# Chunk-selected attention and top-1 routing: the attention loop written out engine by engine

## The chip, the cores and the metric

The program runs on one core of one Trainium2 chip. Its time is the device time of one execution in microseconds (us); the figure for a kernel is the median of its timed runs. The profile is one further execution, seen by the hardware profiler; its span (first to last instruction) is a few us shorter than the device time of the same execution. Engines are named as the profile names them: PE is the matrix engine (PEld its weight loads), DVE the vector engine, ACT the scalar engine, POOL the general engine, SP the one that issues plain transfers.

## The reference

Attention over 4 batches, 8 heads, 768 positions, 64 dimensions, in which each query may look only at the 6 best of 24 chunks of 32 keys; then a mixture of 8 experts of which each token goes to one.

```python
k_min, k_max = min and max of k over each chunk of 32 keys
ub = sum_d max(q*k_min, q*k_max)                 # one bound per query and chunk
ub = where(causal chunk, ub, -1e9); top_chunks = the 6 largest
scores = q @ k.T / 8, kept where the key's chunk is chosen and key <= query
attn = softmax(scores); out = attn @ v           # (4, 8, 768, 64)

x = out as (3072, 512)                           # heads side by side
logits = x @ w_gate; e = argmax(logits); g = softmax(logits)[e]
result[token] = g * relu(x @ w1[e]) @ w2[e]      # (3072, 512)
```

## The kernel before

The attention is done in 16 steps, one for each *pair* of heads (four pairs make a batch). A pair's work is cut into 7 score units; `u` 0 and 1 belong to the first 384 queries, 2 to 6 to the second. Units 1 and 6 have two parts, 256 and 128 queries wide; the others are 384 wide. Scores are computed as keys x queries, exponentiated, cut by the causal mask on POOL, and then used in two ways: as moving operand of the product with v ("AV", `po`), and summed on DVE into an accumulator `acc`, whose column sums give the softmax denominator.

```python
def scores(i, u):                                # 128 columns (keys) at once, bf16
    kte, qsb = KTE[i % 2], QSB[i % 2]            # two key buffers, two query buffers
    ps = ps_s.tile([128, 2, 512], FP32)          # ps_s: two of these
    for (kb, w, c0) in parts: for hd in range(2):
        matmul(pv[:, hd, :], lhsT=kte[:, hd, ts(kb, 128)], rhs=qsb[:, hd, w queries])
    for each part: nc.scalar.activation(P, pv, AF.Exp)
    on diagonal blocks: nc.gpsimd.affine_select(P ...)      # causal

def attend(i, u):                                # 64 columns (dimensions of v), fp32
    for parts, hd: matmul(po[64*hd:64*hd+64, ...], lhsT=vt[:, kb, hd, :], rhs=P[:, hd, ...])
    if last: ot = copy of po (DVE)
    if not first: for parts: nc.vector.tensor_tensor(acc, acc, P, ALU.add)

def ud(i):                                       # 32 columns, fp32
    for hd, hf: matmul(pu[32*(2*hd+hf):+32], lhsT=dcol, rhs=acc[hf][:, hd, :])   # denominators
    for hd, hf: matmul(pu[32*(2*hd+hf):+32], lhsT=wgb[:, hp, hd], rhs=ot[hf])    # gate logits
```

Beside these a pair needs: transposes of its keys (`k0`, `k1`), of its queries (`q0`, `q1`), of the chunk bounds (`select`), of `ud` (`lgp`) and of the two outputs (`x0`, `x1`), all 128-column fp32 transposes in threes; transposes of the chunk mask (`mask`, 64 columns, bf16); and the bounds themselves:

```python
def kse(): KS = kmx + kmn; KD = kmx - kmn        # DVE
def q_e(hf):
    qT = copy of pt (DVE); qA = Abs(pt) (ACT)
    QSB head 0 <- qT (POOL); QSB head 1 <- pt (ACT)
def ub(): pu = KS.T @ qT + KD.T @ qA             # 64 columns, fp32; twice the reference's bound
```

All transposes and `ub`, `ud` share three PSUM buffers (`ps_m`). The loop runs PE in written order; DVE, ACT and POOL are ordered by a scheduler. Pair `i` is interleaved with the preparation of pairs `i+1` and `i+2` and with the outputs of `i-1` and `i-2`:

```python
groups = [(0, 1), (2, 3), (4, 5), (6,)]
for i in range(16):
    for g in range(4):
        g 0: scores(i, 2); scores(i, 3); x1 of i-2
        g 1: scores(i, 4); scores(i, 5); select of i+1; (second pair of a batch) rank
        g 2: scores(i, 6); k0 of i+2; mask of i+1
        g 3: lgp, x0 of i-1; scores(i+1, 0); scores(i+1, 1); k1, q0, q1 of i+2; load k, q, v of i+3
        for u in groups[g]: attend(i, u)
        g 0: ub of i+1; (second pair) logits        g 1: ud of i-1
        (second pair of a batch) g 2: scatter(0, 2, 4)   g 3: scatter(1, 3, 5)
        now and then: load_w of 512 KB of expert weights (POOL queue)
```

Every fourth pair, when a batch is complete, its tokens are routed: `logits` (11 small DVE operations), `rank` (12 small matmuls, 6 small DVE operations) and six scatters of token rows to DRAM (POOL queue). The row buffers `xrow` are three; a batch needs two, so the second buffer of a batch is the one from which the previous batch's scatters 0, 2, 4 read.

After the loop come 28 expert tiles of 128 tokens. A tile is gathered (POOL queue), transposed by a transfer (SP queue), and goes through `up` (8 matmuls of 512 columns), a relu on ACT, a second transfer-transpose, `down` (8 more), a scaling on ACT, and a scatter to the output. The first 11 tiles hold rows of the first three batches and may be gathered before the last batch is routed:

```python
gather(0..3), x_in(0..3) in the last pair; then
up(0); ud; gather(4); up(1); lgp, x0, x1, logits; gather(5); up(2); down(0); rank; gather(6)
scatter(0..5 of the last batch); table(False)
for j in 3..: gather(j + 4); up(j); x_in(j + 3); down(j - 2)
```

Of the kernel before, what the change touches and what calls it, by code (L numbers as in the profile page):

```python
# [24 lines left out]
def kernel(  # L25
# [33 lines left out]
    DC = E  # L59
    NU = 7  # L60
# [36 lines left out]
    wgb = const.tile([128, HP, 2, 32], FP32)  # L97
    tokid = const.tile([128, B, 2, 3], I32)
    warm = const.tile([128, 1], FP32)
    KTE, QSB, KS, KD = [], [], [], []  # L100
    for i in range(2):
        KTE.append(buf.tile([128, 2, S], BF16, name=f"KTE{i}"))
        QSB.append(buf.tile([128, 2, S], BF16, name=f"QSB{i}"))
        KS.append(buf.tile([128, 64], FP32, name=f"KS{i}"))
        KD.append(buf.tile([128, 64], FP32, name=f"KD{i}"))
    nsel = buf.tile([128, 3, 2, 2, 32], BF16, name="nsel")
    colc = work.tile([128, S], BF16, tag="Pa", bufs=4, name="colc")
# [43 lines left out]
    def consts_pool():  # L151
# [3 lines left out]
        zero_half(QSB[1])  # L155
        nc.gpsimd.memset(ones_b[:], 1.0)
# [9 lines left out]
    def consts_last():  # L166
# [3 lines left out]
        nc.sync.dma_start(out=wgb[0:64, :, 0, 0:E], in_=wg_v[0:64])  # L170
        nc.sync.dma_start(out=wgb[64:128, :, 1, 0:E], in_=wg_v[64:128])
# [21 lines left out]
    def load(i):  # L193
        b, hp = divmod(i, HP)
        for nm, src in (("k", k), ("q", q), ("v", v)):
            t_ = ld.tile([128, NT, 2, D], FP32, tag=nm, bufs=2 if nm == "v" else 1)
            for hd in range(2):
                nc.sync.dma_start(out=t_[:, :, hd, :],
                                  in_=src[b, 2 * hp + hd].rearrange("(t p) d -> p t d", p=128))
            st[i][nm] = t_  # L200

    def prep_steps(i):
        s = st[i]
        kte, qsb, ks, kd = KTE[i % 2], QSB[i % 2], KS[i % 2], KD[i % 2]
        kmx = {}
# [7 lines left out]
        def k_e(hf):  # L213
            if hf == 0:
                s["kmx"] = work.tile([128, NCH], FP32, tag="kmx", name="kmx")
                s["kmn"] = work.tile([128, NCH], FP32, tag="kmn", name="kmn")
            pt = s[f"kp{hf}"]
            pk = pt[:].rearrange("p (c w) -> p c w", w=CH)
            nc.vector.tensor_reduce(s["kmx"][:, ts(hf, 12)], pk, AX.X, ALU.max)
            nc.vector.tensor_reduce(s["kmn"][:, ts(hf, 12)], pk, AX.X, ALU.min)  # L220
            nc.scalar.activation(kte[0:64, 0, ts(hf, 384)], pt[0:64, :], AF.Copy, bias=0.0, scale=0.125)  # L221
            nc.scalar.activation(kte[0:64, 1, ts(hf, 384)], pt[64:128, :], AF.Copy, bias=0.0, scale=0.125)

        def k_half(hf):
            k_t(hf)
            k_e(hf)
# [7 lines left out]
        def q_e(hf):  # L234
            pt = s[f"qp{hf}"]
            qT = work.tile([128, 384], FP32, tag=f"qT{hf}")
            qA = work.tile([128, 384], FP32, tag=f"qA{hf}")
            nc.vector.tensor_copy(out=qT[:], in_=pt[:])  # L238
            nc.scalar.activation(qA[:], pt[:], AF.Abs)
            nc.gpsimd.tensor_copy(out=qsb[0:64, 0, ts(hf, 384)], in_=qT[0:64, :])  # L240
            nc.scalar.activation(qsb[0:64, 1, ts(hf, 384)], pt[64:128, :], AF.Copy)
            s[f"qT{hf}"], s[f"qA{hf}"] = qT, qA

        def first():
            s["kmx"] = work.tile([128, NCH], FP32, tag="kmx", name="kmx")
            s["kmn"] = work.tile([128, NCH], FP32, tag="kmn", name="kmn")
            pk = [ps_m.tile([128, 384], FP32, tag="m", name="pk") for _ in range(2)]
            pq = [ps_s.tile([128, 2, 512], FP32, tag="s", name="pq") for _ in range(2)]
            for p_, nm in ((pk, "k"), (pq, "q")):
                for hf in range(2):  # L250
                    dst = p_[hf][:, 0, :] if nm == "q" else p_[hf]
                    for t in range(3):
                        nc.tensor.transpose(dst[:, ts(t, 128)], s[nm][:, 3 * hf + t], ident_f[:])

            def k_red(hf):
                v_ = pk[hf][:].rearrange("p (c w) -> p c w", w=CH)
                nc.vector.tensor_reduce(s["kmx"][:, ts(hf, 12)], v_, AX.X, ALU.max)
                nc.vector.tensor_reduce(s["kmn"][:, ts(hf, 12)], v_, AX.X, ALU.min)

            def k_out(hf, hd):  # L260
                nc.scalar.activation(kte[0:64, hd, ts(hf, 384)], pk[hf][64 * hd:64 * hd + 64, :],
                                     AF.Copy, bias=0.0, scale=0.125)

# [6 lines left out]
            for hf in range(2):  # L270
                s[f"qT{hf}"] = work.tile([128, 384], FP32, tag=f"qT{hf}", name="qT")
                s[f"qA{hf}"] = work.tile([128, 384], FP32, tag=f"qA{hf}", name="qA")
                nc.scalar.activation(s[f"qA{hf}"][:], pq[hf][:, 0, 0:384], AF.Abs)
                nc.vector.tensor_copy(out=s[f"qT{hf}"][:], in_=pq[hf][:, 0, 0:384])
                nc.gpsimd.tensor_copy(out=qsb[0:64, 0, ts(hf, 384)], in_=s[f"qT{hf}"][0:64, :])
            for hf in range(2):
                nc.scalar.activation(qsb[0:64, 1, ts(hf, 384)], pq[hf][64:128, 0, 0:384], AF.Copy)
            k_out(1, 1)

        def select_first():  # L280
# [3 lines left out]
            prep[1]["k0t"]()  # L284
# [29 lines left out]
            scores(0, 0)  # L314
            scores(0, 1)
# [306 lines left out]
    XB = 8  # L622
# [223 lines left out]
```

## Time and profile before

| | us |
|---|---|
| device time, median of 3 (381.53 to 382.80) | 382.76 |
| span of the profiled execution | 375.4 |
| PE busy | 340.7 |
| ACT busy | 236.3 |
| DVE busy | 230.9 |
| POOL busy | 178.3 |
| first AV matmul starts at | 24.5 |
| `ud` of the second-to-last pairs start at (from the matrix engine's timeline) | 241.34, 254.19 |
| first expert matmul starts at | 260.7 |

The table is read from the page's first part and from the timeline of PE. PE is the busiest engine, but its busy time is modelled, and it includes every gap that is shorter than the modelled tail of a matmul; how long a group of matmuls really holds PE is better read from the *starts* in the timeline: the start of the next group minus its own. In the page's strip of 40 slices one slice is 9.4 us, somewhat less than one pair.

Starts of `ud` give the pair's period. In order, from the timeline, the steps between them are 14.48, 14.19, 14.19, 14.68, 16.49, 14.18, 14.19, 14.67, 18.19, 14.18, 14.18, 14.68, 18.10, 12.84 and 8.34 us: a steady 14.2, with a longer step in each of three pairs, those in which a batch is routed.

### The profile page before, as it was taken

The numbers are of one execution on the slowest core, as the hardware profiler recorded it, in microseconds if no ns is written. First come the engines' busy times: TensorE is split into PE (matmuls) and PEld (weight loads), VectorE is DVE, ScalarE is ACT, GpSimd is POOL, SyncE is SP. The second block draws the span as 40 slices with busy tenths as digits, with TensorE's granted clock in tenths as the row PEclk, the third lists the DMA queues.
The fourth block names the chain that finished last, engine by engine and source line by source line (L and its number), as shares of the span: only waits on it lengthen the run. The fifth ranks groups of instructions, "written<-read, shape, count | busy, mean of one in ns | idle before, by whom it ended". The sixth has DMA issues, their size and how long they took to land.

```text
span 375.4 us, 7367 instructions
## 1 busy us (share of the span) xinstructions
PE 340.7 (91%) x2233; PEld 171.5 (46%) x2233; DVE 230.9 (61%) x789; ACT 236.3 (63%) x398; POOL 178.3 (47%) x299
## 2 busy tenths in 40 slices
PE   6778999999988999998999997988997899999980
PEld 3334455465554554553545544443543444444430
DVE  7378798898997888996889898876430000000000
ACT  4467697797785977975779779461453345454430
POOL 3422352352476433548334428467177565555331
PEclk9759999999999999998999999899999999999996
DMA  9455989989979989869898993515799999899750
GB/s 181 73 110 88 182 157 154 190 165 164 177 158 200 181 156 189 164 130 197 158 211 150 167 197 75 113 34 123 97 220 193 248 227 194 202 203 194 183 140 28
DMA packets 138182, 59.81 MB, mean 159 GB/s; under 512 B 122779, under 2 KB 130973, under 8 KB 138144
## 3 DMA queue, kind: packets, MB, share of 16 engines
q1 hardware_dynamic: 120608, 29.91, 42.5%
q0 software_dynamic: 17536, 29.42, 40.2%
q8 instruction: 20, 0.33, 0.3%
q14 instruction: 18, 0.15, 0.1%
HBM read 56.14 MB, written 10.51 MB: 178 GB/s over the span
## 4 chain that ended last, share of the span: by engine, by line
PE 54%; ACT 13%; DVE 10%; issue 9%; DMA 7%; POOL 4%; SPq 1%; POOLq 0%; ACTq 0%; DVEq 0%
PE po L408 14%; PE ps L386 7%; PE ph L659 7%; PE pu L330 6%; PE py L675 5%; ACT Pr L391 3%; PE pt L468 3%; DMA xg<-xs_dram,grow 3%; PE pu L436 3%; ACT QSB L359 3%; ACT QSB L358 3%; PE pu L441 3%; PE pt L231 2%; POOL out_dram L680 2%; DVE Pa L420 2%
## 5 line engine op out<-in xcount | busy, mean ns | idle before, releaser
L420 DVE TENSOR_TENSOR Pa<-Pa,Pr 128x768 f32<-128x768 f32 (+2 forms) x112 | 82.2, 734 | 2.7 <-POOL Pr L395 1.6
L395 POOL TENSOR_SCALAR_AFFINE_SELECT Pr<-Pr 128x256 f32<-128x256 f32 x80 | 34.2, 446 | 73.7 <-ACT Pr L391 72.7
L391 ACT ACTIVATE Pr<-ps 128x768 f32<-128x768 f32 (+2 forms) x112 | 65.3, 628 | 3.5 <-PE ps L386 2.0
L675 PE MATMUL py<-w_all,hT 128*128 x224 | 52.8, 379 | 1.4 <-DMA hT<-h__4677 1.2
L386 PE MATMUL ps<-QSB,KTE 128*128 128x384 bf16 (+2 forms) x288 | 49.4, 296 | 2.0 <-ACT QSB L359 1.1
L680 POOL DMA_INDIRECT out_dram<-y,ti x28 | 27.8, 993 | 38.0 <-ACT y L679 32.5
L386 PEld LDWEIGHTS <-KTE 128*128 128x128 bf16 x288 | 24.4, 99 | 33.9 <-issue 26.1
L675 PEld LDWEIGHTS <-hT 128*128 128x128 bf16 x224 | 21.9, 98 | 28.2 <-DMA hT<-h__4677 1.6
L533 POOL DMA_INDIRECT xs_dram<-xrow,sli x24 | 26.4, 1101 | 13.8 <-DVE sli L526 5.2
L659 PE MATMUL ph<-w_all,KTE 128*128 x120 | 28.4, 379 | 3.6 <-DMA KTE<-xg 3.3
L444 ACT ACTIVATE ud<-pu 128x384 f32<-128x384 f32 x16 | 7.9, 491 | 35.0 <-PE pu L441 32.5
L391 ACT ACTIVATE Pa<-ps 128x768 f32<-128x768 f32 x32 | 26.0, 811 | 2.3 <-PE ps L386 1.6
L659 PE MATMUL ph<-w_all,QSB 128*128 x104 | 24.6, 379 | 0.0
L186 POOL DMA_DIRECT2D w_all<-in_moe_w_dram x32 | 24.4, 762 | 0.0
L240 POOL CAST QSB<-qT 64x384 bf16<-64x384 f32 x30 | 14.9, 505 | 14.3 <-DVE qT L238 13.9
L647 DVE TENSOR_TENSOR ti<-xg,inv_i 128x1 int32<-128x1 int32 x9 | 1.5, 172 | 30.4 <-DMA xg<-xs_dram,grow 30.4
L470 DVE TENSOR_TENSOR xrow<-pt,rec 128x384 bf16<-128x384 f32 x32 | 17.6, 552 | 4.1 <-DMA xs_dram<-xrow,sli 3.3
L659 PEld LDWEIGHTS <-KTE 128*128 128x128 bf16 x120 | 11.6, 98 | 18.2 <-DMA KTE<-xg 3.1
L630 POOL DMA_INDIRECT xg<-xs_dram,grow x16 | 16.9, 1057 | 4.8 <-issue 3.5
L413 DVE COPY ot<-po 128x384 f32<-128x384 f32 x32 | 17.7, 554 | 2.4 <-PE po L408 2.2
L679 ACT ACTIVATE y<-py,xg 128x512 f32<-128x512 f32 x16 | 11.0, 687 | 12.8 <-PE py L675 10.4
L221 ACT ACTIVATE KTE<-pt 64x384 bf16<-64x384 f32 x30 | 14.5, 483 | 6.2 <-DVE kmn L220 5.8
(317 smaller groups left out, 654.6 us busy)
## 6 DMA issues: line engine op xcount, KB each, us to landing
w_all<-in_moe_w_dram POOLq DMA_DIRECT2D x32, 512.0 KB, 7.2
out_dram<-y,ti POOLq DMA_INDIRECT x28, 3.7
t__119<-in_k_dram SPq DMA_DIRECT2D x2, 192.0 KB, 3.2
t__122<-in_q_dram SPq DMA_DIRECT2D x2, 192.0 KB, 3.9
t__125<-in_v_dram SPq DMA_DIRECT2D x2, 192.0 KB, 4.3
t__134<-in_v_dram SPq DMA_DIRECT2D x2, 192.0 KB, 4.2
t__128<-in_k_dram SPq DMA_DIRECT2D x2, 192.0 KB, 3.4
t__131<-in_q_dram SPq DMA_DIRECT2D x2, 192.0 KB, 4.1
```

Of the source, the lines that this page charges most:

```text
L186: d = nc.gpsimd.dma_start(out=dst, in_=src.rearrange("(c p) f -> p c f", p=128))
L330: nc.tensor.matmul(pu[64 * hf:64 * hf + 64, :], lhsT=w_[:], rhs=s[f"{nm}{hf}"][:], start=(nm == "qT"), stop=(nm == "qA"), skip_group_check ...
L386: nc.tensor.matmul(pv[:, hd, :], lhsT=kte[:, hd, ts(kb, 128)], rhs=qsb[:, hd, ds(qb * 384 + 384 - w, w)], start=True, stop=True, skip_grou ...
L391: nc.scalar.activation(P[:, :, ds(c0, w)], pv, AF.Exp)
L395: nc.gpsimd.affine_select(out=pd, in_=pd, pattern=[[0, 2], [1, 128]], compare_op=ALU.is_ge, fill=0.0, base=0, channel_multiplier=-1)
L408: nc.tensor.matmul(po[64 * hd:64 * hd + 64, 384 - w:384], lhsT=vt[:, kb, hd, :], rhs=P[:, hd, ds(c0, w)], start=first, stop=last and n == ...
L413: nc.vector.tensor_copy(out=ot[:], in_=po[:])
L420: nc.vector.tensor_tensor(acc[:, :, 384 - w:384], acc[:, :, 384 - w:384], P[:, :, ds(c0, w)], ALU.add)
L533: d = nc.gpsimd.indirect_dma_start(out=xs_dram[:], out_offset=bass.IndirectOffsetOnAxis(ap=sli[:, u:u + 1], axis=0), in_=bst[b][f"xrow{u % ...
L659: nc.tensor.matmul(ph[:, fh, :], lhsT=xT[:, c, :], rhs=w_all[:, ds(wo + (c * F + fh * 512), 512)], start=(c == 0), stop=(c == NDC - 1), sk ...
L675: nc.tensor.matmul(py[:], lhsT=hT[:, c, :], rhs=w_all[:, ds(wo + (W1W + c * DM), DM)], start=(c == 0), stop=(c == NFC - 1))
L680: d = nc.gpsimd.indirect_dma_start(out=out[:], out_offset=bass.IndirectOffsetOnAxis(ap=fs[j]["ti"], axis=0), in_=y[:], in_offset=None, bou ...
```

## The change

Six things are done, and all of them in the attention loop or at the seam behind it.

1. **Scores on 64-column tiles.** Each score matmul is split in two, 64 keys each, written to the lower and upper half of the PSUM tile; they then have the same column width as AV.
2. **A new order of PE.** Scores and AV alternate unit by unit; the 128-column transposes are collected in three visits per pair: keys; then `ud`, output and bounds; then output and queries. Preparation is split into steps so that PE, DVE and ACT parts can be placed apart.
3. **Written order on DVE and ACT too** in the loop, not PE alone; in the expert part too.
4. **Three key buffers** instead of two.
5. **Work moved.** Unit 6 is no longer added to the accumulator on DVE; `ud` sums it with further `dcol` matmuls, and needs only two gate matmuls, as both heads' gate columns now stand side by side in `wgb`. The bound is rewritten as k_min·q + (k_max - k_min)·relu(q): `KS` is a copy, and relu(q) is made on POOL from `qT`, where |q| was made on ACT.
6. **The seam.** `logits` moves to the first pair after a batch, `rank` to the start of the second; scatters go out one per slot; eight tiles are gathered in the last pair instead of four; the last batch's scatters go out two at a time between expert tiles; k, q and v are loaded separately, each as its buffer is freed.

The core of the diff, with cuts marked:

```diff
-    for i in range(2):
+    for i in range(3):
         KTE.append(buf.tile([128, 2, S], BF16, name=f"KTE{i}"))
...
-            nc.scalar.activation(qA[:], pt[:], AF.Abs)
+            nc.gpsimd.tensor_scalar(qA[:], qT[:], 0.0, None, ALU.max)
...
-                nc.vector.tensor_tensor(ks[r, c], s["kmx"][r, :], s["kmn"][r, :], ALU.add)
+                nc.vector.tensor_copy(out=ks[r, c], in_=s["kmn"][r, :])
...
-                nc.tensor.matmul(pv[:, hd, :], lhsT=kte[:, hd, ts(kb, 128)],
-                                 rhs=qsb[:, hd, ds(qb * 384 + 384 - w, w)], ...)
+                for c in range(0, 128, CW):                     # CW = 64
+                    nc.tensor.matmul(pv[c:c + CW, hd, :], lhsT=kte[:, hd, ds(kb * 128 + c, CW)],
+                                     rhs=qsb[:, hd, ds(qb * 384 + 384 - w, w)], ...)
... (ud)
+            for n, (kb, w, c0) in enumerate(parts):             # parts of unit 6
+                for hd in range(2):
+                    if n == 0:
+                        mm(2 * hd, wgb[:, hp, :], s[f"ot{hd}"][:], start=False, stop=True)
+                    mm(2 * hd + 1, dcol[:], s["P6"][:, hd, ds(c0, w)], w, ...)
... (the loop; cut: k, q, v loads, weights, first and last pairs)
+            av(i - 1, 6); out_t(i - 1, 1); scores(i, 0); scores(i, 1)
+            r["ud"](); pn["q_v"](1); scatters(i, 0)
+            if hp == 1 and b > 0: route[b - 1]["rank"]()
+            keys(j, lambda: scores(i, 2))                       # visit 1
+            if hp == 1 and b > 0: route[b - 1]["rank_v"]()
+            av(i, 0); scores(i, 3); scatters(i, 1); av(i, 1); add(i, 1); out_t(i, 0)
+            pn["ub"](); pj["kse"](); scatters(i, 2)
+            r["lgp_t"](); r["x_t"](0); pn["select_t"]()         # visit 2
+            r["lgp"](); r["xr"](0); pn["select"]()
+            scores(i, 4); av(i, 2); scores(i, 5); av(i, 3); scatters(i, 3)
+            scores(i, 6); add(i, 3)
+            if hp == 0 and b > 0: route[b - 1]["logits"]()
+            r["x_t"](1); pj["q_t"](0); pj["q_t"](1)             # visit 3
+            r["xr"](1); add(i, 4); scatters(i, 4)
+            pn["mask"](); av(i, 4); pj["q_v"](0); pj["q_s"](0); pj["q_s"](1)
+            add(i, 5); av(i, 5); scatters(i, 5)
... (expert tiles)
-                    if lo == 0 and j + 4 < hi:
-                        gather(j + 4)
+                    if lo == 0 and j + 5 < hi:
+                        if late:
+                            r["scatter"](late[:2]); del late[:2]
+                        gather(j + 5)
```

Here `r` stands for the outputs of pair i-1, `pn` for the preparation of i+1, `pj` for that of i+2, `hp` for the pair's place in its batch (0 to 3); `xr(hf)` multiplies the transposed output by the reciprocal denominators into `xrow`, on DVE.

## The prediction

> **What bounds the kernel now.** I read the page's strip first, then busy time by stretch, then the PE timeline of one steady pair, then the stretches that are longer.
>
> ```profile
> PE   6778999999988999998999997988997899999980
> PEclk9759999999999999998999999899999999999996
> ```
>
> PE is busy nearly everywhere; the 7 and 5 at the left are the start-up, and its granted clock dips twice more, at the two 8s (around 170 and 240 us), which are batch seams. Busy time by stretch: a steady pair, then one in which a batch is routed (columns: stretch, its length, busy us of PE, PEld, DVE, ACT, POOL, PE clock, DMA share, GB/s).
>
> ```profile
> 133.16:147.35 14.19, 14.11 (x111) 7.57 (x109) 12.53 (x40) 11.64 (x21) 5.30 (x13) 1.00 0.91 168
> 162.02:180.21 18.19, 16.04 (x111) 8.07 (x109) 13.90 (x48) 11.83 (x21) 12.65 (x17) 0.91 0.85 176
> ```
>
> In the steady pair PE has no hole, DVE is at 88% (12.53 of 14.19), ACT at 82%: PE sets the pace. So I ask what PE's 14.19 us consist of (start, modelled us, group; I subtract starts).
>
> ```profile
> 138.11 0.82 PE L386 MATMUL ps<-QSB,KTE 128*128 128x384 bf16 x6
> 138.77 0.52 PE L210 MATMUL pt<-ident_f,t__1772 128*128 128x128 f32 x3
> ...
> 142.64 0.82 PE L408 MATMUL po<-Pr,t__1570 128*64 128x256 f32 x8
> 143.29 0.82 PE L330 MATMUL pu<-qT,KS 128*64 128x384 f32 x4
> 143.94 0.82 PE L330 MATMUL pu<-qA,KD 128*64 128x384 f32 x4
> 144.69 0.84 PE L386 MATMUL ps<-QSB,KTE 128*128 128x384 bf16 x4
> 145.43 0.55 PE L338 MATMUL pt<-ident_f,ubT 128*128 128x128 f32 x3
> 145.91 0.87 PE L408 MATMUL po<-Pa,t__1570 128*64 128x384 f32 x4
> 146.60 0.81 PE L408 MATMUL po<-Pr,t__1570 128*64 128x384 f32 x4
> ```
>
> Units: one AV unit 0.65 (142.64 to 143.29); two score units 0.66 (138.11 to 138.77), so 0.33 each; `ub` 2 x 0.65. The second half of `ub` takes 0.75 (143.94 to 144.69) where the first took 0.65: leaving 64 columns for 128 cost 0.10. Going back costs as much again: three transposes hold PE 0.48 (145.43 to 145.91) ahead of AV, but 0.38 where scores follow (137.73 to 138.11 in the same timeline), and the AV unit behind them takes 0.69 instead of 0.65. A change of column width is thus 0.10 to 0.14 us.
>
> **What the Trainium skill says.** "TensorEngine Tiling (Array Packing)", section Tiling Modes, states that changing the mode, not just the tile, drains the engine: that is the 0.10 to 0.14 us. The same page, Tile-to-Partition Mapping, Restrictions, says that column tiling switches fast weight load off: narrower scores could pay in their loads. The trace shows the loads close together, 98 ns for 128 columns of bf16 keys and 109 ns for 64 of the mask:
>
> ```profile
> L386 PEld LDWEIGHTS <-KTE 128*128 128x128 bf16 x288 | 24.4, 99 | 33.9 <-issue 26.1
> ...
> L356 PEld LDWEIGHTS <-nsel 128*64 128x64 bf16 x90 | 5.4, 109 | 3.2 <-issue 1.7 <-DVE nsel L349 0.9 <-DVE Pa L420 0.5
> ```
>
> "TensorE: Matmul & The Clock Gate", Part 3, says matmuls in different column groups run at the same time. The trace agrees: `ub` gives four matmul passes of 384 columns per 0.65 us in two groups, and `ud` eight in 0.67 in four groups. So two 64-column halves should cost what one 128-column score matmul does. The same page, Part 1, says the clock halves after an idle window of some 3.4 us; here a hole of 1.82 us before AV at 173.18 is enough: it is followed by a half of `ub` that takes 1.29 us (175.01 to 176.30) instead of 0.65.
>
> **The change part by part.**
>
> *Steady pair.* Work that stays: 7 AV x 0.65 = 4.55; 7 scores x 0.33 = 2.31; `ub` 1.30; `ud` 0.67 + 0.66 = 1.33 (afterwards the second half is two gate matmuls beside the `dcol` sums of unit 6 in other groups, 384 columns deep as before); 24 transposes x 0.11 = 2.64; mask 0.30. Sum 12.43. The other 1.76 us of 14.19 are nine changes of width (32 to 128, then 64, 128, 64, 128, 64, 128, 64, 32), about 9 x 0.12 = 1.1, and 0.65 of short waits and exposed weight loads. Afterwards the widths run 64, 32, 128 (keys), 64, 128 (second visit), 64, 128 (third), 64: seven changes, 7 x 0.13 = 0.9, and an allowance of 0.2 for weight loads that stay exposed. 12.43 + 0.9 + 0.2 = 13.5; I take 13.6. Gain 0.6 a pair, over some 15 pairs **9 us**.
>
> *Do DVE and ACT keep up?* DVE loses unit 6's additions, 0.70 + 0.43 a pair; ACT loses |q|, 14.7 us over the loop or 0.9 a pair:
>
> ```profile
> L420 DVE TENSOR_TENSOR Pa<-Pa,Pr 128x512 f32<-128x512 f32 x32 | 22.4, 701 | 2.2 <-POOL Pr L395 1.6 <-PE po L408 0.4
> L420 DVE TENSOR_TENSOR Pa<-Pa,Pr 128x256 f32<-128x256 f32 x32 | 13.7, 428 | 0.2
> L239 ACT ACTIVATE qA<-pt 128x384 f32<-128x384 f32 x30 | 14.7, 488 | 0.4
> ```
>
> That leaves DVE 11.4 and ACT 10.7 of 13.6. POOL gets relu(q), estimated from its cast of half that height (0.5 us each) as 1.2 a pair, on 5.3. All fit. The critical placing on ACT is the two mask copies (0.80 each) followed by the two query copies (0.49) ahead of the next pair's first exp: about 2.6 us behind PE's mask transposes, while PE has two AV, the last AV and one score unit (2.3 us) to do; the exp is then 0.3 late, and PE uses its result only some 2 us later. No stall, but little room.
>
> *Batch seams, three of them.* Before, the longer steps are 16.49, 18.19 and 18.10, plus 0.3 to 0.5 in the pair ahead: 12 us in all over the steady step. Afterwards `logits` (11 DVE operations of 0.15 to 0.2 us, some 1.7 us) falls in a pair with about 1.3 us of slack: excess 0.4. In the second pair `rank` adds 0.3 on PE. Then one wait that I think gets worse: `xr(1)` of that pair writes the buffer which scatters 0, 2, 4 still read. The trace has their landing and the same wait before:
>
> ```profile
> DMA to landing us min/median/max: 6.6/6.8/7.0
> ```
> ```profile
> 173.73 0.56 DVE L470 TENSOR_TENSOR xrow<-pt,rec 128x384 bf16<-128x384 f32 x1 [1.26 <-DMA xs_dram<-xrow,sli]
> ```
>
> Before, that product ran in the pair after; now it comes in the same pair. I lay DVE's written order out with its steps in the timeline (0.47 for a reduction, copy or output product, 0.86 for a 768-wide addition, 1.0 for unit 1's two, 1.9 for a selection): the key transposes give the first reduction at 3.2 us into the pair, four of them end at 5.1, `rank` at 5.8; additions, copy, `kse` (0.7), `lgp` (0.35), `xr(0)`, selection and addition 3 are 5.7 more, so `xr(1)` is due at about 12. Row numbers are ready at 5.8; POOL then needs three issues of 1.1 us, in one seam with a weight load and a small sum between, so the third starts at 8 to 9 and lands 6.8 later, at 15 to 16. DVE waits 3 to 4, and `ud` of the next pair, which needs the last addition, some 0.7 less. With a halved clock behind it (about 1.3 us), a seam costs 4 to 5: 12 to 15 in all. Gain **-2**.
>
> *Last two pairs.* PE's waits there before (1.4, 0.7, 1.1 us) go partly: **+1.5**.
>
> *Expert part.* PE is at its floor but for one hole:
>
> ```profile
> 291.92 1.24 PE L659 MATMUL ph<-w_all,KTE 128*128 x5 [3.32 <-DMA KTE<-xg]
> ```
>
> Tile 7's gather stood behind six scatters on POOL. Now eight tiles are gathered before, and later gathers stand behind two scatters at a time: **+3.5**. 224 + 224 matmuls of 216 ns and the last transfers stay.
>
> *Start.* One more mask row fill on DVE, one more memset on POOL, keys of pair 1 loaded earlier: 0.
>
> Sum 9 - 2 + 1.5 + 3.5 = 12, and 382.8 - 12 = 370.8. I add 0.7 for stalls of three engines in fixed order: **371.5 us**.
>
> **The rivals.**
>
> (a) *Fixed order stalls.* Once DVE or ACT is late, nothing else may overtake. For it: the ACT placing above has 0.3 us of room, and the scatter wait blocks all of DVE. Against: both have 2 us or more free per pair. It would keep the pair at 14.2 and lengthen seams: 376 to 383.
>
> (b) *Narrow scores cost more than they save.* Twice as many loads, and parts 128 wide stream in 50 ns (five mask transposes of that width in 0.25 us) against loads of 109. If alternating bf16 scores and fp32 AV cost 0.05 each, 12 times a pair is 0.6 and the loop gains nothing: 378 to 380. Against: mask transposes (bf16, 64 columns) go straight into AV in this trace without a visible gap.
>
> (c) *Transfers become the bound.* DMA share is 0.91 in the steady pair and would be 0.95 at 13.6. For it: query loads take up to 9.7 us. Against: no PE wait in the loop names a load of k, q or v, and each is needed a whole pair after its buffer is free. It would give 374 to 377.
>
> (d) *Better than I think.* If all 0.65 us of waits go and the scatter lands in time, pairs of 13.4 and seams of 2 us each: 362.
>
> **Range and chances.** (d) gives the low end, 362; (a) or (b) with lost seams the high end, 383. Faster by over 2% means under 375.1; my 371.5 leaves 3.6 us, about what one wrong seam or 0.25 us a pair takes away: 0.65. Within 2%: 0.25. Slower: 0.10, for a stall per pair that I don't see.
>
> **What would show it.** Steps between `ud` starts of 13.5 to 13.8; score units of 0.33 in 64 columns; seven changes of 0.1; no hole of 3 us among the expert tiles; in each routing pair a DVE wait of 3 to 4 us on the scatter at `xr(1)`. I am wrong if the steps are 14 or more with PE waiting on ACT or DVE in every pair, or if score units take 0.4.

## The result, and the profile after

The changed kernel took 398.9 us (398.2 to 400.8) where the kernel before took 382.8 (381.5 to 383.0) on the same chip: a ratio of 1.044 (95% interval 1.039 to 1.048). The prediction was 371.5 us, with a range of 362 to 383. On another chip, where the kernel before takes 375.9, the changed kernel took 390.7: 1.039 (1.032 to 1.046). Chips differ by up to 2% here, so experiments are compared by their ratio to the kernel before on the same chip, and by steps in their traces. The profile of the kernel before that the first part reads is of an execution of 377.1 us, not of 382.8: its column below belongs beside that of the second chip.

Three marks on PE's timeline cut the span into start, attention and expert part (us; "second chip" is the unchanged changed kernel run again there):

| | before | after | after, second chip |
|---|---|---|---|
| first AV | 24.5 | 22.6 | 22.6 |
| attention: first AV to first expert matmul | 236.2 | 253.6 | 251.8 |
| expert part, to the end | 114.7 | 121.0 | 113.9 |
| span | 375.4 | 397.3 | 388.2 |

The expert part's 121.0 is not the change's: the same program has 113.9 on the second chip. Every expert part that was profiled on chips where the kernel before takes 376 or so lay between 111.9 and 115.3, and the 114.7 of the kernel before is one of that kind. The time was lost in the attention.

The strip of the page after, PE and its granted clock (40 slices of 9.9 us):

```profile
PE   5688999998689997959998878876997898899990
PEclk9779999999989999999999899988998999999996
```

Where PE's line of before fell to 7 once in the loop, this one has an 8, a 6 and an 8 around 105 us, a 7 and a 5 at 154 and 174, and from 208 us on 8, 8, 7, 8, 8, 7, 6 up to the first expert tile.

Busy time by stretch, with the columns of the prediction's table: a steady pair, the first pair that scatters a batch, and the last pair up to the first expert tile.

```profile
129.16:143.21 14.05, 13.41 (x133) 8.78 (x130) 11.83 (x37) 10.85 (x20) 8.66 (x15) 1.00 1.05 194
94.26:115.13 20.87, 15.51 (x145) 10.04 (x142) 12.59 (x43) 11.17 (x21) 15.92 (x22) 0.92 0.89 171
255.48:276.30 20.82, 13.95 (x94) 6.18 (x91) 10.46 (x35) 5.85 (x10) 12.55 (x16) 0.84 0.34 76
```

The steady pair is hardly shorter (14.05 for 14.19), and PE now has a hole in it. In the routing pair and in the last pair PE is idle for 5 to 7 us while no other engine is full.

In order, the steps between `ud` starts after are 14.37, 14.12, 14.05, 16.03, 20.87, 14.05, 14.05, 16.00, 18.88, 14.05, 14.18, 17.87, 18.75, 12.50 (and 22.60, which contains the first expert tile). What ends PE's waits, the longest entries of that view (waited for, us in all, times, longest):

```profile
PE pt L345 <- DVE xrow L467: 20.4, 13, 5.3
PE po L395 <- POOL Pr L382: 3.4, 3, 1.5
```

The first line is 20 us in all and new. L345 is the mask transposes, L467 is `xr(1)`, and neither computes anything for the other. What ties them is PSUM: in visit 3 `x_t(1)`, `q_t(0)` and `q_t(1)` take all three `ps_m` buffers, and the mask needs a fourth; it gets the one of `x_t(1)`, when `xr(1)` has read it. `xr(1)` stands in DVE's queue behind `add(3)`, so in a steady pair (DVE's and PE's timeline):

```profile
138.54 1.16 DVE L407 TENSOR_TENSOR Pa<-Pa,Pr 128x768 f32<-128x768 f32 x1
139.63 0.55 DVE L467 TENSOR_TENSOR xrow<-xp,rec 128x384 bf16<-128x384 f32 x1
```
```profile
138.39 0.55 PE L463 MATMUL xp<-ident_f,ot 128*128 128x128 f32 x3
138.77 0.82 PE L230 MATMUL pt<-ident_f,q 128*128 128x128 f32 x6
140.22 0.44 PE L345 MATMUL pt<-ident_b,nsel 128*64 128x128 bf16 x5 [0.64 <-DVE xrow L467]
```

PE has done `x_t(1)` by 138.9, but DVE is in an addition until 139.6, and the mask starts at 140.2 with 0.64 us lost. In a pair with hp 0 the 11 operations of `logits` stand in between as well (step 16.0). In a pair with hp 1 the same product waits for the scatter that still reads its row buffer, here in the first of the three:

```profile
110.09 0.56 DVE L467 TENSOR_TENSOR xrow<-xp,rec 128x384 bf16<-128x384 f32 x1 [4.06 <-DMA xs_dram<-xrow,sli]
```
```profile
110.71 0.69 PE L345 MATMUL pt<-ident_b,nsel 128*64 128x128 bf16 x5 [5.29 <-DVE xrow L467]
111.09 0.90 PE L395 MATMUL po<-Pr,v 128*64 128x384 f32 x1
111.19 0.31 PE L345 MATMUL pt<-ident_b,nsel 128*64 128x128 bf16 x1
111.30 3.26 PE L395 MATMUL po<-Pr,v 128*64 128x384 f32 x15
```

DVE waits the predicted 4 us, and PE waits 5.3. The 16 AV matmuls behind it then take 3.2 us (111.1 to 114.3) where the steady pair takes 2.0 (140.45 to 142.44): the granted clock is 0.50 from 111 to 113. In the other two routing pairs DVE waits 1.55 and 1.5 us for the scatter, PE 2.8 and 2.7 for the buffer and then 1.5 more for a mask on POOL.

### The profile page after: what moved, and what is told of

Read it like the earlier page. It is cut to its first block, busy times and chain, and to the rows that moved or that the text cites. A ratio compares the mean times of both kernels' runs of the same rounds, so it can differ in the third digit from the quotient of the medians.

```text
span 397.3 us, 7968 instructions
## 1 busy us (share of the span) xinstructions
PE 336.4 (85%) x2575; PEld 189.3 (48%) x2585; DVE 220.0 (55%) x759; ACT 224.5 (56%) x368; POOL 228.7 (58%) x330
## 4 chain that ended last, share of the span: by engine, by line
PE 32%; DVE 24%; POOL 18%; issue 14%; DMA 4%; ACT 3%; another core or an unknown queue 2%; SPq 1%; POOLq 0%; ACTq 0%; DVEq 0%
PE po L395 8%; PE ph L664 7%; DVE Pa L407 6%; POOL qA L237 5%; PE py L680 5%; POOL xs_dram L534 3%; PE pu L422 3%; PE ps L373 3%; DVE top L335 3%; POOL out_dram L687 2%; PE pu L316 2%; DMA KTE<-xg 2%; DVE xrow L467 2%; DVE kmn L221 1%
## 5 line engine op out<-in xcount | busy, mean ns | idle before, releaser
L407 DVE TENSOR_TENSOR Pa<-Pa,Pr 128x768 f32<-128x768 f32 (+2 forms) x80 | 66.2, 827 | 13.3 <-PE ps L373 5.4
L395 PE MATMUL po<-Pr,v 128*64 128x384 f32 (+2 forms) x448 | 67.1, 419 | 3.4 <-POOL Pr L382 3.4
L373 PE MATMUL ps<-QSB,KTE 128*64 128x384 bf16 (+2 forms) x576 | 56.2, 302 | 4.0 <-ACT Pr L378 3.4
L237 POOL TENSOR_SCALAR qA<-qT 128x384 f32<-128x384 f32 x30 | 43.0, 1434 | 24.9 <-DVE qT L236 24.7
L382 POOL TENSOR_SCALAR_AFFINE_SELECT Pr<-Pr 128x256 f32<-128x256 f32 x80 | 42.0, 541 | 25.4 <-ACT Pr L378 25.0
L395 PEld LDWEIGHTS po<-Pr,v 128*64 128x64 f32 x448 | 36.6, 144 | 22.9 <-POOL Pr L382 9.6
L373 PEld LDWEIGHTS <-KTE 128*64 128x64 bf16 x576 | 32.2, 112 | 30.4 <-issue 28.2
L224 ACT ACTIVATE KTE<-pt 64x384 bf16<-64x384 f32 x64 | 30.9, 483 | 11.8 <-PE pt L212 8.1
L220 DVE TENSOR_REDUCE kmx<-pt 128x12 f32<-128x384 f32 x32 | 17.8, 557 | 23.7 <-PE pt L212 19.3
L395 PE MATMUL po<-Pa,v 128*64 128x384 f32 x128 | 27.8, 516 | 2.1 <-POOL Pa L382 2.1
L687 POOL DMA_INDIRECT out_dram<-y,ti x14 | 14.1, 1004 | 22.0 <-ACT y L686 16.0
L345 PE MATMUL pt<-ident_b,nsel 128*64 128x128 bf16 x90 | 8.1, 230 | 21.1 <-DVE xrow L467 20.4
```

The lines of the kernel that those rows point to most:

```text
L224: nc.scalar.activation(kte[0:64, hd, ts(hf, 384)], s[f"kp{hf}"][64 * hd:64 * hd + 64, :], AF.Copy, bias=0.0, scale=0.125)
L237: nc.gpsimd.tensor_scalar(qA[:], qT[:], 0.0, None, ALU.max)
L373: nc.tensor.matmul(pv[c:c + CW, hd, :], lhsT=kte[:, hd, ds(kb * 128 + c, CW)], rhs=qsb[:, hd, ds(qb * 384 + 384 - w, w)], start=True, stop ...
L382: nc.gpsimd.affine_select(out=pd, in_=pd, pattern=[[0, 2], [1, 128]], compare_op=ALU.is_ge, fill=0.0, base=0, channel_multiplier=-1)
L395: nc.tensor.matmul(s["po"][64 * hd:64 * hd + 64, 384 - w:384], lhsT=vt[:, kb, hd, :], rhs=P[:, hd, ds(c0, w)], start=first, stop=last and ...
L407: nc.vector.tensor_tensor(acc[:, :, 384 - w:384], acc[:, :, 384 - w:384], P[:, :, ds(c0, w)], ALU.add)
```

## The experiments

Theory: waits that fixed queues put on PE (the mask behind DVE's order; later also POOL's order) are the loss. Rival A: 64-column scores cost more than they bring. Rival B: POOL's additional work, the relu of 1.43 us a time, is the loss. Rival C: transfers bind the routing pairs. Edits are to the changed kernel unless said; ratios are to the kernel before on the same chip (changed kernel: 1.044 and 1.039). The experiments ran in four groups, each on one chip, in the order below; the kernel before took 382.9, 376.8, 375.9 and 375.7 us there.

### The table later

```diff
-            if i == NP - 2: table(True)      # at the end of pair 14
+                if i == NP - 1: table(True)  # pair 15, behind r["ud"]()
```

> The routing table of the early tiles, some 4.1 us of small DVE operations, is written behind ud of pair 14 instead of ahead of out_t of pair 14; nothing else moves. Written-order theory (the loss is made of waits that the fixed order of DVE puts on PE): the hole of 3.35 us in ud of pair 14 closes, and with it part of the slow stretch behind it; 3 to 8 us less than the changed kernel, 391 to 396 us. Rival A (64-column scores and their width changes cost the time): no effect, 398 to 400. Rival B (engine work, POOL's longer relu above all): no effect, since no work is removed.

Measured: 400.0 us, ratio 1.046 (1.041 to 1.052), nothing won, which is what the rivals had foretold; from `ud` of pair 14 to the first expert tile it is still 20.9 us. The hole in `ud` (2.86 us in the changed kernel) is gone, and two others stand in its place (PE's waits):

```profile
PE po L395 <- POOL Pr L382: 5.4, 2, 4.6
PE po L395 <- DVE rec L446: 2.6, 1, 2.6
```

AV now waits for what stands behind the table in DVE's queue, and for masks on POOL. The hole was real and not the one that counted; what held this stretch, the runs further down show.

### `xr(1)` earlier in DVE's queue

```diff
             scores(i, 6)
-            add(i, 3); logits (hp 0)
             r["x_t"](1); pj["q_t"](0); pj["q_t"](1)
             r["xr"](1)
+            add(i, 3); logits (hp 0)
             add(i, 4)
```

> DVE's order alone: xr(1) is written ahead of add(3) and of logits, so that the PSUM buffer which the mask transposes need comes free earlier; no operation is added or removed. Written-order theory: the wait of the mask for xrow loses about 0.7 us in each steady pair and about 2.3 us in each of the three pairs with logits, and the pairs with a scatter keep theirs (the scatter's landing ends it): 8 to 13 us less, 386 to 391 us; pairs with hp 0 from 16.0 to about 14.2 us. Rival A (narrow scores) and rival B (POOL's relu): within 1 us of 399.

Measured: 394.2 us, ratio 1.031 (1.025 to 1.036). The steady pair falls from 14.05 to 13.5 (13.65, 13.45, 13.54), the pair with `logits` from 16.0 to 14.3 to 14.5, as expected. Of 13 waits of the mask three are left, those on scatters:

```profile
PE pt L345 <- DVE xrow L467: 11.7, 3, 5.6
```

The routing pairs got longer, though (23.0, 20.3, 19.7), so only 5 of 8 to 13 us arrived: DVE reaches `xr(1)` earlier and waits longer for the same landings, 11.0 us in three pairs where the changed kernel has 7.1. This shows the mechanism in the steady pair, and that PE's own need is what the prediction said.

### `xr(1)` of the routing pairs in the next pair

```diff
-            if i: r["x_t"](1)  ...  r["xr"](1)
+            if i and not (hp == 1 and b > 0): r["x_t"](1)  ...  r["xr"](1)
+            if hp == 2 and b > 0: rout[i-2]["x_t"](1); rout[i-2]["xr"](1)   # behind visit 1
```

> In the three pairs whose xr(1) stands behind the landing of a scatter, x_t(1) and xr(1) are moved into the next pair, behind its keys; nothing else moves. Written-order theory: the waits of 4 us on DVE and of 5.3 us on PE in these pairs vanish and with them the half clock behind them: steps of 20.9, 18.9 and 18.8 us become about 14.5 to 15, the next pair gains some 0.3; 10 to 16 us less, 383 to 389 us. Rival C (transfers bound these pairs whatever the order): the wait reappears in another place and less than 4 us is won. Rivals A and B: no effect.

Measured: 397.0 us, ratio 1.038 (1.033 to 1.043), a miss. The wait on the scatter is gone, and the first routing pair falls from 20.9 to 16.2 as expected, but the other two stay at 19.5. The 1.9 us won are under the 4 that rival C allowed, so the time alone would fit it; the waits do not name a transfer. What holds the two pairs, in POOL's timeline of the second:

```profile
161.10 1.35 POOL L534 DMA_INDIRECT xs_dram<-xrow,sli  x1 [1.07 <-DVE base_e L528]
162.75 1.02 POOL L534 DMA_INDIRECT xs_dram<-xrow,sli  x1 [0.30 <-issue]
164.07 0.97 POOL L534 DMA_INDIRECT xs_dram<-xrow,sli  x1 [0.30 <-issue]
165.03 0.83 POOL L188 DMA_DIRECT2D w_all<-in_moe_w_dram  x1
...
166.35 1.55 POOL L534 DMA_INDIRECT xs_dram<-xrow,sli  x1 [0.18 <-issue]
168.21 0.98 POOL L534 DMA_INDIRECT xs_dram<-xrow,sli  x1 [0.30 <-issue]
169.19 0.44 POOL L382 TENSOR_SCALAR_AFFINE_SELECT Pr<-Pr 128x256 f32<-128x256 f32 x1
169.80 1.68 POOL L534 DMA_INDIRECT xs_dram<-xrow,sli  x1 [0.18 <-issue]
171.47 0.79 POOL L382 TENSOR_SCALAR_AFFINE_SELECT Pr<-Pr 128x256 f32<-128x256 f32 x2
```

The causal masks (L382) of units 5 and 6 stand behind five and six scatters of 1.0 to 1.7 us. AV of unit 5 starts at 169.68, straight behind the first mask. PE's waits for POOL in this kernel are 14.0 us in 10 places. So there is a second queue, largely hidden until the first was cleared; POOL's own count shows it, too, 15.92 us of work in the 20.87 us pair above, which is more than the 13.5 us PE needs.

### Scores back in 128 columns

```diff
-    CW = 64
+    CW = 128
```

> The scores go back to 128 columns of TensorE, two matmuls in place of four for each unit, with the new order of everything kept. If changes of width cost what they did in the kernel before (about 0.12 us each, and the weave of scores with AV now makes some ten more of them in a pair): up to 1.2 us more in a pair that PE sets, part of it hidden in the waits of the mask; 8 to 18 us more than the changed kernel, 407 to 417 us. Rival A (64-column scores are themselves the loss): 5 to 20 us less. If the waits of the written order set the pair whatever PE's work is: within 3 us of 399.

Measured: 398.1 us, ratio 1.040 (1.033 to 1.047): no difference from the changed kernel; its steady pair is 14.04. The third outcome: the width doesn't matter while waits set the pair, because what PE loses in width changes it would have waited anyway: the mask's 13 waits for `xr(1)` become 6 (16.0 us), and those of the steady pairs are gone. Rival A falls, and so does a gain from narrow scores in this order.

### The relu on ACT

```diff
-            nc.gpsimd.tensor_scalar(qA[:], qT[:], 0.0, None, ALU.max)
+            nc.scalar.activation(qA[:], s[f"qp{hf}"][:], AF.Relu)
```

> One part alone: the relu of the queries is made by ACT from PSUM (about 0.5 us each on ACT, two a pair) in place of POOL's 1.43 us each. Rival B (POOL's work is the loss, since POOL also makes the causal masks for which AV waits, and issues the scatters and gathers): 8 us or more less, 391 us or below, and the waits of AV for POOL shrink everywhere. Written-order theory (DVE's order holds the mask back, POOL only adds to it): 1 to 5 us less, 394 to 398 us; the wait of the mask for xrow stays at about 20 us in all.

Measured: 400.9 us, ratio 1.062 (1.058 to 1.067). POOL's busy time falls from 229 to 189 us and the kernel gets 2% slower, which neither theory had expected. POOL's busy time as such is not the loss, so rival B in its plain form is gone; what the relu costs in POOL's queue this run can't weigh, since the edit brings in a wait of its own. The steady pair grows by 0.8, to 14.84, and the new wait appears in 13 pairs: the queries' PSUM tile is now held until ACT's relu, which is written behind the copy of `ud`, and the key transposes (L212) wait for a buffer:

```profile
PE pt L345 <- DVE xrow L467: 21.3, 13, 5.4
PE po L395 <- POOL Pr L382: 7.6, 4, 4.4
PE pt L212 <- ACT ud L436: 6.6, 13, 0.7
```

### Four gathers in the last pair; six scatters in one go

```diff
# first kernel
-                for n in range(8): gather(n) ...      # pair 15
+                for n in range(4): gather(n) ...      # 4, 5, 6 behind ud, logits, rank; then gather(j + 4)
# second kernel
+            r["scatter"](late); late = []             # ahead of table(False)
```

> The issue of the row gathers alone goes back to the order of the kernel before: four in the last pair and the others spread over the first expert tiles, in place of eight in the last pair; the late scatters stay where the change has them. If eight gathers in a row on POOL (about 1.3 us each) hold back the causal masks of the last pair: the stretch from ud of pair 14 to the first expert tile falls from 20.8 us by 3 to 6 us. If the hole behind that stretch is something else: under 1 us there. The expert part itself may lose up to 3 us, since gathers come later. In all 393 to 399 us.

> The six scatters of the last batch are issued in one go ahead of the second table, as in the kernel before, in place of two ahead of each of three gathers; the eight early gathers stay. If the late scatters between gathers make the holes of the expert part (121.0 us against 114.7): the expert part loses 3 to 6 us, 393 to 396 us. If its holes come from something else (ACT's and DVE's order, issue): within 1.5 us of 399, or slower if the scatters in a row hold the output scatters back.

Measured: 1.033 (1.029 to 1.038) and 1.041 (1.034 to 1.048), against 1.039 (1.032 to 1.046) of the changed kernel in the next group. Attention 251.7 and 251.6, expert part 113.7 and 114.7, where the changed kernel has 251.8 and 113.9: neither edit does anything that can be told apart. The first didn't do what it was meant to: POOL is ordered by the scheduler, and eight gathers still stand ahead of the last masks in its trace, from 259.66 to 270.5. So it leaves the seam open; the second says that the scatters' order is not what the expert part lives on.

### Three repairs with the relu on ACT

```diff
  xr(1) earlier + xr(1) of routing pairs in the next pair + relu on ACT
```

> Three repairs of the attention loop at once: xr(1) ahead of add(3) and logits, x_t(1) and xr(1) of the scatter pairs moved into the next pair, and the relu on ACT, so that POOL has 2.9 us a pair more room for masks and scatters. Written-order theory with POOL as the next in line: steady pairs at 13.4 to 13.7 us, pairs with logits about 14.4, pairs with scatters 15 to 16.5 in place of 19 to 21; attention 18 to 22 us shorter, in all 377 to 382 us, about level with the kernel before. If the scatter pairs are bound by the transfers themselves, they stay at 18 or more, and the sum is 386 to 390 us. Rival A (narrow scores): over 392 us.

Measured: 393.5 us, ratio 1.044 (1.040 to 1.049), a miss. Steady pairs 14.2 to 14.4, routing pairs 18.0, 21.1, 21.4; the waits for ACT's `ud` copy are back (6.7 us), and those for POOL's masks are 12.0 us. Taking 2.9 us a pair of relu from POOL didn't clear its queue in the routing pairs, since six scatters still lie in it.

### The changed kernel again, and POOL in written order

```diff
# second kernel
-    MAN = {PE, DVE, ACT}
+    MAN = {PE, DVE, ACT, POOL}
```

> The changed kernel itself, unchanged, beside the other kernels of this group, as their yardstick, since the kernel before took 383 us on one chip and 377 on another. If the longer expert part (121.0 us against 114.7) belongs to the change: it is again 5 us or more over what the repaired kernels of the group have, and the ratio to the kernel before is again 1.04. If it belongs to the chip: the expert part here is as long as in the other kernels of the group.

> POOL alone is put into written order, as PE, DVE and ACT are; nothing else moves. It is then known that in the last pair its eight gathers stand behind the last causal masks, where the scheduler had put them ahead. POOL-order theory (the masks wait behind gathers and scatters in POOL's queue): the stretch from ud of pair 14 to the first expert tile falls from 20.8 by 3 to 6 us, and the scatter pairs gain 0 to 2 us each: 4 to 9 us less than the changed kernel. If DVE's order alone is at fault: within 1.5 us of it, or slower, as POOL then waits in its own order.

Measured: again 390.7 us; its steps in the loop are those of the first profile within 0.2 us but for two (22.7 for 20.9, 16.3 for 17.9), and the expert part is shorter by 7.1 us. In the first profile the matmuls of one `up` came singly, some 0.7 us apart, and it took 5.9 us in place of 1.7, while the engine waited for nothing that the profile shows. The four profiles of the first group (where the kernel before takes 383) have an `up` of 5.1 to 6.2 us there too, two of them with single matmuls and two with a wait of 2.5 us for ACT behind it; those of the other groups have none. Why is open; it isn't the change.

POOL in written order: 398.1 us, ratio 1.060 (1.051 to 1.069), a miss, and worth reading. PE's waits for POOL's masks are no longer among its longest. It waits for the other end of the same queue:

```profile
PE pt L345 <- DVE xrow L467: 27.6, 13, 6.7
PE ph L663 <- DMA KTE<-xg: 7.2, 1, 7.2
```

Scatters that now stand behind masks are issued later and land later, so `xr(1)` waits longer; gathers that stand behind the last mask let the first expert tile wait 7.2 us for its rows. Order alone can't help while the work is too much for its stretch or too late for its use.

### Six scatters over two pairs; then POOL in order too

```diff
# first kernel: xr(1) earlier and deferred as above, relu on POOL, and
-        n = 6 * (hp - 1) + slot - 1           # hp 1: five, hp 2: one
+        n = 3 * (hp - 1) + slot - hp          # hp 1: slots 1 to 3, hp 2: slots 2 to 4
# second kernel: the same, POOL in written order, table(True) in pair 15
```

> DVE's order repaired (xr(1) ahead of add(3) and logits; xr(1) of the scatter pairs in the next pair), POOL keeps its relu, and the six scatters of a batch are spread over two pairs, three each, in place of six in one. Theory of two queues (DVE's order holds the mask back, and in the scatter pairs POOL, with some 8 us of scatters on top of its 10 us a pair, holds AV back): steady pairs at 13.5 us, pairs with logits 14.4, pairs with scatters 14 to 15.5 and the ones behind them about 14: attention about 20 us shorter than the changed kernel's, in all 16 to 22 us less. If the scatter pairs are bound by the landing of the transfers: they stay at 17 or more, and 8 to 12 us are won.

> The repaired order with spread scatters, POOL in written order, and the table of the early tiles behind ud of pair 14. If both queues were the loss, the last pair too is a plain one: 20 to 27 us less than the changed kernel, 1 to 3 per cent under the kernel before. If something else holds the last pair: no better than the kernel with spread scatters alone.

Measured: 383.7 us, ratio 1.020 (1.012 to 1.027), and 380.2 us, 1.012 (1.009 to 1.015): 7.0 and 10.4 us less than the changed kernel, well short of the 16 to 22 and 20 to 27 expected. The first has steady pairs of 13.65 to 13.75 and routing pairs of 17.2, 19.2 and 20.6; the scheduler still puts scatters ahead of masks. With POOL in written order these become 16.9, 17.0, 17.1, and attention is 241.2 where the changed kernel has 251.8. What is left over the kernel before sits in the last pair:

```profile
265.14 0.59 PE L663 MATMUL ph<-w_all,KTE 128*128 x1 [7.97 <-DMA KTE<-xg]
```
```profile
255.05 0.77 POOL L382 TENSOR_SCALAR_AFFINE_SELECT Pr<-Pr 128x256 f32<-128x256 f32 x2 [1.24 <-ACT Pr L378]
256.15 1.40 POOL L634 DMA_INDIRECT xg<-xs_dram,grow  x1 [0.34 <-issue]
```

The first gather is issued at 256.2, behind the last mask, and PE, done with attention at 257.2, waits 8 us for its landing and its transpose.

### The last pair

```diff
  as the last kernel, but
+                if i == NP - 2: table(True)   # visit 1 of pair 14, its scratch tile in a buffer of its own
+            early(i, lo, hi)                  # pair 15: gather 0 behind score unit 3, 1-2 behind ub, 3-4 behind unit 6, 5-7 at the end
+        for n in range(4): x_in(n)            # behind the last out_t
   scatter slots: hp 1: 1, 2, 4; hp 2: 1, 2, 3
```

> As the kernel with everything repaired (380.2 us), and the last pair too: the table of the early tiles stands in the visit 1 of pair 14, where no keys are made any more, the eight gathers stand between the causal masks of pair 15 instead of behind them, and what waits for their landing on DVE stands behind the last out_t. If the chain table, gather, landing holds the first expert tile back (8 us in the kernel with everything repaired): up(0) comes 5 to 8 us earlier, 372 to 376 us, level with the kernel before or up to 1 per cent faster. If the gathers between the masks hold POOL up again: no gain.

Measured: 369.9 us, ratio 0.990 (0.984 to 0.996): faster than both kernels, than the one before by 1%. Steps of steady pairs 13.43 to 13.64, routing pairs 15.1, the pairs behind them 16.2, and from `ud` of pair 13 to the first expert tile 27.0 us instead of 35.2. Attention is 230.0 us, 6.2 less than before. The strips of its page:

```profile
PE   5678999999998999999899999899799999999980
PEclk9869999999999999999999999999999999999997
```

The clock has no dip left between the start and the end. Three things were moved at once for the last pair, and the scatters' slots with them; they weren't separated.

The routing pairs themselves gained little: one and the pair behind it take 31.3 us together, 31.6 in the kernel with everything repaired, and two steady pairs take 27.1. In the second of them `xr(1)`, moved there, still waits for the scatter to land:

```profile
172.71 0.56 DVE L467 TENSOR_TENSOR xrow<-xp,rec 128x384 bf16<-128x384 f32 x1 [2.26 <-DMA xs_dram<-xrow,sli]
```

So rival C stands in a weak form: the landing of a scatter holds part of these pairs. How much of the 4.2 us it explains no run shows.

### What the width of scores is worth

```diff
# first kernel: the one with the last pair repaired, CW = 128
# second kernel: the kernel BEFORE, each score matmul in two of 64 columns, nothing else
# third kernel: the one with the last pair repaired, relu on DVE (nc.vector.tensor_scalar)
```

> The same with scores in 128 columns, two matmuls in place of four a unit. By PE's order 12.2 changes of width a pair in place of 7.4; at about 0.12 us each 0.55 us a pair, 9 us in all, if PE sets the repaired pairs. The steady pair then goes from 13.5 to about 14.0, the sum up by 5 to 9 us. Rival A (narrow scores cost more than they bring): it is faster than with 64 columns. If something else than PE sets the repaired pairs: within 2 us.

> One part of the change alone, on the kernel before: scores in 64 columns, order and everything else of the kernel before. Its order has the scores beside 128-column transposes, so that the changes of width rise from 9.3 a pair to 11.3: about 0.24 us a pair, 2 to 5 us in all over the kernel before, 0.5 to 1.3 per cent slower. Rival A (narrow scores themselves are the loss of the change): 3 to 5 per cent slower. If the width of scores matters by the work they do: faster.

> The kernel with the last pair repaired, and the relu of the queries on DVE (SBUF to SBUF) in place of POOL's 1.43 us each. If POOL still holds AV back in the scatter pairs: these lose 1 to 2 us each and PE's waits for POOL fall by half; steady pairs stay at 13.5 if DVE has room, or rise by up to 0.7 us if DVE, with two more operations of some 0.4 us a pair, is what sets them. In all between 4 us less and 6 us more.

Measured: 378.6 us, ratio 1.010 (1.006 to 1.014); 380.8 us, 1.014 (1.008 to 1.021); 374.8 us, 0.996 (0.994 to 0.999).

Once the waits are gone, width counts: 128 columns cost 8.7 us, of which 1.8 stand ahead of the first AV (which moved by 1.3 between kernels of one width, too); the steady pairs rise by 0.5 to 1.2 us (to 14.01, 14.12 and, once, 14.83). By PE's timeline a steady pair of that kernel has 12 changes of width for 7, so 0.10 to 0.12 us each in the two lower ones. In the kernel before, 64 columns *cost* 0.32 us a pair (14.19 to 14.51), for 12 changes in place of 9 (the expectation counted two more, the timeline shows three): 0.11 us each. So the narrow tile brings nothing by itself; the gain is in having fewer changes, and needs the new order.

The relu on DVE takes 366 ns there where POOL takes 1434, yet the kernel is slower than with POOL's: steady pairs rise from 13.5 to 14.2 and more. DVE is then busy for 12.37 of 14.18 us (11.33 of 13.43 with POOL's relu), and its additions come later: the weight loads of `ud` wait for them in 14 pairs, 12.8 us in all, and a steady pair's `ud` takes 2.2 us where it took 1.5. POOL's slow relu is the better place.

## Why the prediction was wrong, point by point

1. **Steady pair, 14.19 to 13.6, gain 9: the sum was right, the pair was not.** 12.43 of work and seven changes of width do give 13.5, as the runs with `xr(1)` moved and with the last pair repaired show (13.4 to 13.65). Measured in the changed kernel: 14.05, because the mask waits 0.64 us. Gain 0.14 x 15 = 2 instead of 9. The units were right, too (PE's timeline of the changed kernel, score unit 0.32, AV unit 0.65, by their starts):

```profile
132.43 0.49 PE L373 MATMUL ps<-QSB,KTE 128*64 128x384 bf16 x4
132.75 0.82 PE L395 MATMUL po<-Pr,v 128*64 128x256 f32 x8
133.40 0.81 PE L316 MATMUL pu<-qT,KS 128*64 128x384 f32 x4
```


2. **The step that failed: "DVE waits 3 to 4, and `ud` of the next pair, which needs the last addition, some 0.7 less."** The wait's size was right in the first routing pair (4.06; 1.55 and 1.5 in the others). Its victim was not. I followed only data from DVE to PE, and there the next user is `ud`. The nearer user was of the *buffer*: three PSUM tiles were in flight, the mask needed the first back, and it stands 3 us ahead of `ud` (140.2 and 143.25 in the steady pair). I had DVE's order, with `add(3)` and `logits` ahead of `xr(1)`, laid out in steps, and asked of each only when its result is needed, not when its input tile is. The same step explains point 1 and the pairs with `logits` (excess over 14.05: 2.0, predicted 0.4).

3. **Seams, excess 12 to 15 us.** Over the pairs with hp 0 and 1 the excess before was 11.7 (1.5 and 10.2); on the second chip after it is 24.3 (6.2 and 18.1). That is 12.6 us lost for a predicted 2. That two of the routing pairs of the first profile, with 4.8 and 4.7 over the steady pair, lie in the predicted 4 to 5 is luck: there DVE's wait is 1.5, PE's 2.8 and 2.7, a mask on POOL adds 1.5, and the clock doesn't fall.

4. **"All fit" for POOL was checked in the steady pair alone.** There 8.66 of 14.05 fits. A routing pair had 12.65 us of POOL already, and the relu, estimated at 1.2 a pair, takes 2 x 1.43 = 2.9; 15.92 were measured. Queues then hold AV back, which the repairs showed only after DVE's order was cleared.

5. **Last two pairs, +1.5.** As a remainder: 15.6 us more attention on the second chip, less 12.6 of seams, plus 2 of steady gain, are 5 us lost. The first AV came 1.9 us earlier, for a predicted 0. The prediction didn't follow the chain from table over gathers to the first tile, nor that eight gathers share a queue with masks. Placing table and gathers otherwise won 8.2 us from `ud` of pair 13 on.

6. **Expert part, +3.5.** The hole of 3.3 us did go, but other short waits came (1.7 on a transpose of `hT` the longest): 113.9 for 114.7, so 0.8. The 121.0 of the first profile is the chip's.

7. **Rivals.** (a), stalls of the fixed order, is what happened, and at 399 beyond its own 383. (b) is refuted by the units above and by the run with 128 columns, and (c) isn't borne out: the repaired kernels move the same bytes in 13.4 us pairs. (d) isn't reached: the last repaired kernel, whose routing pairs still cost 4.2 us a batch, is 1% faster than before, where 362 would have been 5%. Whether the scheduler, left to order DVE, would have placed `xr(1)` early enough by itself wasn't tried.

The term for width rested on the Trainium skill's "TensorEngine Tiling (Array Packing)", section Tiling Modes, that a change of mode drains the engine, and it holds: 0.10 to 0.12 us for a change where 128 columns came back, 0.11 where 64 came into the kernel before. What was missing rests on the Trainium skill's "PSUM — Partial Sum Buffer", section Engine vs sequencer instructions, which says that the queues of ACT, DVE and GpSimd are strictly first in, first out: `xr(1)`, whose input is there by 138.9, starts at 139.6, when the addition ahead of it is done.

## What to carry to other kernels

Before an engine's order is fixed by hand, follow each buffer as well as each value: for every tile of a small pool, ask which operation frees it, what stands ahead of that operation in its queue, and who takes the tile next. Add up each engine's work in the heaviest stretch, not in the steady one, as a queue that is too full there delays whatever stands in it. And when a saving is real but the time doesn't move, clear one queue at a time: here each wait showed only when the one ahead of it was gone.

## What the runs showed of the hardware

- POOL's relu of 128 x 384 fp32 took 1.15 to 1.23 us in the changed kernel's loop, but 1.79 to 1.85 in each of the 12 places where an addition of two SBUF tiles had begun on DVE some 0.2 us before it. Such an addition of 768 columns took 0.94 to 1.04 us there, and 1.16 where a mask had begun on POOL just before it (138.47 and 138.54). The Trainium skill's "SBUF — State Buffer", section SBUF: two separate sides, says that the two engines share a pair of ports and lock each other out, DVE with two SBUF inputs among them; 0.6 us more on an operation of 1.17, for the one that began second, agrees with that.
- Chips differed mainly in one stage: the same program's expert part took 121.0 us on one and 113.9 on another, while a steady pair took 14.05 and 14.04. The kernel before took 382.9 us where expert parts of 119.5 to 121.8 were seen, and 375.7 to 376.8 on the others.
- A wait of 5.3 us was followed by a halved clock (16 AV matmuls in 3.2 us for 2.0), and so was one of 2.86 in `ud` of pair 14 (granted clock 0.50 from 261 to 263). The wait's length alone doesn't decide: after 2.0 us at 156.2 and 2.8 us at 173.2 the clock stayed at 1.00, while the 1.82 us that the prediction read were enough. Over four executions each, the mean granted clock was 0.939 to 0.962 in the changed kernel on the second chip and 0.968 to 0.980 in the last repaired one.
